# In the last two attention tiles: half of the first mixings' results in the scores' PSUM banks, and the copy of the second mixing's result one slot earlier, between two exponentials

## The chip, the core and the metric

The kernel runs on one core of a Trainium2 chip. The core has five engines that run side by side, each through its own list of instructions in order: PE (TensorE, matrix products, results into PSUM), DVE (VectorE), ACT (ScalarE), POOL (GpSimd) and SP, which here only issues DMAs. They wait for each other by semaphores. The metric is the device time of one execution in microseconds (us); less is better.

## What is computed

Attention with "talking heads" for 4 batches, 12 heads, 448 positions of 64 elements, and then an MLP with SiLU over the 1792 tokens:

```python
scores = scale * np.matmul(q, k.transpose(0, 1, 3, 2))
scores = np.einsum('bhij,hg->bgij', scores, w_pre)      # first mixing of the heads
scores = scores - np.max(scores, axis=-1, keepdims=True)
attn = np.exp(scores)
attn = attn / (np.sum(attn, axis=-1, keepdims=True) + 1e-09)
attn = np.einsum('bhij,hg->bgij', attn, w_post)         # second mixing
out = np.matmul(attn, v)
h = x @ w_in                                            # x: out, one row per token
g = h * (1.0 / (1.0 + np.exp(-h)))
return g @ w_out
```

## The kernel before, in words

A *tile* is up to 120 query positions of one batch; there are 16 tiles, four to a batch. A tile is worked in *groups* of 10 positions times 12 heads, 12 groups in most tiles and 10 in the last of a batch: 184 groups, 0 to 183. The last two tiles are groups 162 to 173 and 174 to 183.

The loop over the groups is written out as a software pipeline, and the order of its lines is the order of the instructions on each engine; nothing is reordered later. One pass of the loop is a *slot*, i. Groups go in pairs (i, i + 1 with i even), and below "pair i" means this pair. In an even slot the order of the calls is:

- `mix_pair` for pair i + 4 (line 399): 8 matmuls `pp<-g,wpre` on PE, the first mixing of the scores, into two PSUM banks. In the kernel before these come from the pool `ps_p`, which has two banks, so each mixing needs the banks of the pair before it.
- In the last tile (slots from `n_last` = 174) the row maxima `nm<-pp` of both groups (line 405, DVE); in earlier tiles they come a few lines later in the same slot.
- `put_pair` of pair i - 2 (line 446, ACT): one copy `at<-pa` of the result of the second mixing, from the only buffer `pa` for it into the tile's attention matrix.
- `norm_pair` of pair i + 2: a reciprocal on DVE (line 422) and two scalings `wr<-wpost,r` on POOL (line 425).
- the exponential `e<-pp,nm` of group i + 4 (line 409, ACT).
- work spread over the slots by tables: `scores` (line 339, PE, copied out by ACT and DVE at 344 and 346), `values` (line 368, PE, `po<-at,v`, copied out by ACT at 375). The scores and the values take their banks from `ps_m`, four banks used in turn. The last scores are made in slot 162; after it `values` runs in slots 164, 167, 171, 177, 180 and 182.
- `mix_pair_again` for pair i (line 437): 64 small matmuls `pa<-wr,e` on PE into `pa`. It needs `pa` copied out, so the `put_pair` of pair i - 2.

In the odd slot i + 1: the exponential of the pair's second group (i + 5), the copies of `po`, and `bound_sums` (line 418, POOL), which starts what the next slot's `norm_pair` needs.

Beside this the MLP's weights are converted in the background, in units (`convert`). In nearly every pair of slots from 166 on one unit runs: in the even slot DVE L86 and, for the unit before, DVE L63 and POOL L66 (and for every second unit POOL L69 to L72); in the odd slot ACT L90, after the exponential, and then DVE L92 and L93, which use what L90 writes. They come on DVE ahead of the next even slot's row maxima.

In the last slots the MLP begins: L650 and L652 (ACT, DVE) split its first operands in two, L615 and L616 (ACT, POOL) do so for its weights, and in slot 182 its first two products `ph<-op` (line 645) run on PE, one ahead of the last `mix_pair_again` and one behind it. The second needs the weights of the second L616.

Of the kernel before, what the change touches and what calls it, by code (L numbers as in the profile page):

```python
# [103 lines left out]
def talking_heads_then_silu_mlp(  # L104
# [63 lines left out]
    def pool(name, bufs, stack=ctx, **kw):  # L168
        return stack.enter_context(tc.tile_pool(name=name, bufs=bufs, **kw))
# [7 lines left out]
    ps_m = pool("ps_m", 4, late_ps, side="right", space=PSUM)  # L177
# [3 lines left out]
    ps_p = pool("ps_p", 2, mixing, space=PSUM)  # L181
# [5 lines left out]
    def pair(p, tag, dtype=F32R):  # L187
        return p.tile([128, 2, S], dtype, name=tag, tag=tag)
# [7 lines left out]
    def bank(p, name):  # L196
        if p is ps_a:
            turns.append(name)
            return pa[:, len(turns) % 2]
        return p.tile([128, 512], F32, name=name, tag="bank")  # L200
# [158 lines left out]
    def values(n, first_pair, pairs):  # L359

        b, ti = seq[n]
        t0, m, _ = tiles[ti]
        po = bank(banks[0], "po")
        for c in range(pairs):
            h = 2 * (first_pair + c)
            for j in range(NJ):
                for i in range(2):
                    nc.tensor.matmul(  # L368
                        po[i * D:(i + 1) * D, c * m:(c + 1) * m], lhsT=vs[b, h][:, i, j, :],
                        rhs=ats[n][:, j, h + i, :m], start=(j == 0), stop=(j == NJ - 1))  # L370

        def take():
            for c in range(pairs):
                p = first_pair + c
                nc.scalar.copy(
                    out=xt[p // HC, b % 2, p % HC][:, b // 2, t0:t0 + m].rearrange("p (x y s) -> p x y s", y=R, s=2),
                    in_=po[:, c * m:(c + 1) * m].rearrange("p (x s y) -> p x y s", y=R, s=2))
        return [(take, None)]
# [71 lines left out]
    seq = [(b, ti) for b in range(B) for ti in range(len(tiles))]  # L450
# [5 lines left out]
    groups, first = [], []  # L456
# [12 lines left out]
    def put(i, what, *args, lead=0, w=0.0):  # L469
        i = max(i, 0)  # L470
        (early if lead else work)[max(i - lead, 0)].append((what, args))
        sent[max(i - lead, 0)] += w

    NE = 3
    for n in range(1, len(seq)):
        p0, p1 = first[n - 1], first[n]
        spread = (0, 0, 0, 0, 2, 2) if n == 1 else (-6, -5, -4, -2, -1, 0) if p1 - p0 == 12 else (-6, -5, -4, -3, -2, -1)
        for h in range(0 if n > 1 else 2 * NE, H, 2):
            i = p0 + spread[h // 2]
# [7 lines left out]
    for n, (b, ti) in enumerate(seq):  # L487
# [12 lines left out]
        if ti == 0:  # L500
            for h in range(0, H, 4):
                put(first[n] + ((5, 6, 8) if n else (15, 16, 18))[h // 4], load_v_quad, b, h, lead=2, w=1.8)
    n_last = first[len(seq) - 1]
    lighter = set()
    for n in range(2, len(seq) - 1):
        slots = range(first[n], first[n + 1])
# [96 lines left out]
    def load_part(j):  # L603
        src, k, p = parts[j]
        if src is wo_dram:
            for _ in conv:
                pass
        n = p.stop - p.start
        raws[j] = box["w"].tile([128, 4, 128], F32R, name="wl", tag="wl", bufs=WB)[:, :n]
        nc.sync.dma_start(out=raw(raws[j]), in_=src[:, p, k])  # L610

    def ready_part(j):
        wl = raws.pop(j)
        wh = box["w"].tile([128, 4, 128], F32R, name="wh", tag="wh", bufs=WB)[:, :wl.shape[1]]
        nc.scalar.copy(out=wh, in_=raw(wl))  # L615
        nc.gpsimd.tensor_sub(out=wl, in0=raw(wl), in1=raw(wh))  # L616
        ready[j] = wh, wl
# [14 lines left out]
    def product(s, p):  # L632

        kind, k, u, a = steps[s]
        if kind == "o":
            return product_out(s, p)
        nk = HC
        todo = []
        for n in range(nk):
            wh, wl = (x[:, (a * nk + n) % 4] for x in ready[part_of(kind, k, a * nk + n)])  # L640
            x = ops[u][n]
            todo += [(0, wh, x[:, 0]), (1, wh, x[:, 1]), (2, wl, x[:, 0])]
        todo.sort(key=lambda t: t[0])
        for n, (_, w, x) in enumerate(todo):
            nc.tensor.matmul(p[:, :T], lhsT=w, rhs=x, start=(n == 0), stop=(n == len(todo) - 1))  # L645

    def halve(src, dst):

        hi, lo = (dst[:, 0], dst[:, 1]) if not isinstance(dst, tuple) else dst
        nc.scalar.copy(out=hi, in_=src)  # L650
        yield
        nc.vector.tensor_sub(out=lo, in0=src, in1=raw(hi))  # L652
# [42 lines left out]
    for i in range(len(groups) + 1):  # L695
        g, new, old = at(i), at(i + LEAD), at(i - 1)
        if i == n_last:
            early_p.close()
            xw = pool("xw", 1)
            box["w"] = pool("w", 1)  # L700

            ops[0] = [pair(xw, f"op0{c}") for c in range(HC)]
            splits = [halve(xs[0][0, 0, c], ops[0][c]) for c in range(HC)]
        for what, args in early[i]:
            what(*args)
        fresh = [new, at(i + LEAD + 1)] if new and i % 2 == 0 else []
        if fresh:
            new.mix_pair(fresh[1], ps_p)
        if i >= n_last:
            for x in fresh:  # L710
                x.top()
        if new and i % 2:
            new.exp(at(i + LEAD - 1).s[:, 1:2])
        for take, _ in done:
            take()
        if 0 < i < len(groups) and i % 2 == 0:
            at(i - 2).put_pair()
        for take, _ in later:
            if take:
                take()  # L720
        if i == len(groups) - 1:
            old.put_pair()
        if any(what is scores for what, _ in work[i]):
            for _, take in later:
                if take:
                    take()
            later = []
        if i < n_last:
            for x in fresh:
                x.top()  # L730
        for _, take in later:
            if take:
                take()
        if i % 2 and at(i + 3):
            at(i + 3).bound_sums()
        if i % 2 == 0 and at(i + 2):
            at(i + 2).norm_pair(at(i + 3))
        if scaled:
            next(conv)
            scaled = False  # L740
        for take in lows:
            take()
        if fresh:
            new.exp_first()
        later, done, highs, lows = [], [], [], []
        for what, args in sorted(work[i], key=lambda x: order.index(x[0])):
            while len(later) + len(done) + len(lows) + 1 + (what is scores) > 4:
                for take in (done or later).pop(0):
                    if take:
                        take()  # L750
            new_takes = what(*args) or []
            if what in (prep_q, prep_k):
                highs += [take for take, _ in new_takes]
                lows += [take for _, take in new_takes]
                new_takes = []
            if what is scores:
                while len(later) > 1:
                    for take in later.pop(0):
                        if take:
                            take()  # L760
            (done if what is values else later).extend(new_takes)
        for take in highs:
            take()
        if i == len(groups) - 2:
            phs.append(bank(ps_m, "ph"))
            product(0, phs[0])
        if g and i % 2 == 0:
            g.mix_pair_again(at(i + 1))
        if i == len(groups) - 2:
            phs.append(bank(ps_m, "ph"))  # L770
            product(1, phs[1])
        if i >= n_last:
            if i >= n_last + 2 and splits:
                if next(splits[0], 1):
                    splits.pop(0)
            if n_last + 2 <= i < n_last + 2 + WB:
                load_part(i - n_last - 2)
        if i in lighter:
            scaled = next(conv, None)
        if i in (len(groups) - 5, len(groups) - 3):  # L780
            ready_part(len(ready))
# [7 lines left out]
    for h in (0, HH):  # L789
        ready_part(len(ready))  # L790
        banks[:] = [(ps_m, ps_h)[h // HH]]
        new = values(len(seq) - 1, h // 2, HC)[0]
# [166 lines left out]
```

## Time and profile before

| | us |
|---|---|
| time, median of 3 runs | 857.35 (852.56 to 858.68) |
| profiled execution, time | 857.05 |
| profiled execution, span | 855.3 |
| PE busy in the span | 811.6 (95%) |
| DVE busy | 625.6 (73%) |
| ACT busy | 511.0 (60%) |
| POOL busy | 428.5 (50%) |

All times of rows are microseconds from the start of the span; 1.75 us of the profiled execution lie outside it. An L with a number is a line of the kernel, and `out<-in` names the tiles that an instruction writes and reads. "[x <-E t Ln]" behind a row says that the engine sat idle for x us ahead of it, until engine E had done the instruction of line n on tile t. The attention takes the time up to some 435 us, the MLP the rest.

### The profile page before, as it was taken

To read this page: it belongs to the slowest core of one execution; us is meant where nothing else is said; L and a number is where in the kernel's file an instruction comes from. 1 tells how busy PE (TensorE), PEld (TensorE's weight loads), DVE (VectorE), ACT (ScalarE), POOL (GpSimd) and SP (SyncE) were. 2 spreads that over 40 slices of the span, in tenths; PEclk is the share of its full clock that TensorE was granted. 3 is DMA by queue.
4 is the path that set the end of the run, shared out by engine and by line. 5 is a ranking of instruction groups with operands and counts; after the bars stand their busy time and mean duration, and the time that the engine had idled before them with its cause. 6 is when DMAs were issued, how large, how long until landed. Compare 5 with 4: busy or idle time off the path is not lost.

```text
span 855.3 us, 27555 instructions
## 1 busy us (share of the span) xinstructions
PE 811.6 (95%) x11148; PEld 661.6 (77%) x11148; DVE 625.6 (73%) x1137; ACT 511.0 (60%) x1114; POOL 428.5 (50%) x693
## 2 busy tenths in 40 slices
PE   7898999799998999999899999999999999999997
PEld 5455666467665666666599999998989999999996
DVE  5553867467775777675778798999998888787343
ACT  4675878578886888787756554224676533433330
POOL 6131536355553554563877588457644435433440
PEclk9899999899999999999999999999999999999999
DMA  8668678887788786875535346335522122111133
GB/s 172 185 181 190 189 207 232 211 207 208 209 238 225 217 216 203 239 232 160 182 117 177 124 148 200 109 105 154 154 71 66 56 73 90 52 55 56 56 121 130
DMA packets 156839, 132.90 MB, mean 155 GB/s; under 512 B 52164, under 2 KB 150448, under 8 KB 156712
## 3 DMA queue, kind: packets, MB, share of 16 engines
q1 hardware_dynamic: 154339, 129.29, 53.3%
q8 instruction: 88, 1.44, 0.7%
q10 hardware_dynamic: 1956, 1.19, 0.6%
q0 software_dynamic: 416, 0.66, 0.3%
q14 instruction: 40, 0.32, 0.1%
HBM read 64.01 MB, written 27.53 MB: 107 GB/s over the span
## 4 chain that ended last, share of the span: by engine, by line
PE 71%; DVE 12%; DMA 6%; ACT 4%; issue 3%; POOL 2%; SPq 1%; ACTq 1%; DVEq 0%; POOLq 0%
PE ph L645 17%; PE ph L629 12%; PE pt L629 9%; PE pa L437 9%; PE po L368 7%; PE pp L399 7%; PE pqk L339 7%; DMA g<-st 3%; DVE op L652 2%; ACT e L409 1%; DVE nm L405 1%; DVE g L836 1%; DVE cg L92 1%; ACT at L446 1%; DVE g L838 1%
## 5 line engine op out<-in xcount | busy, mean ns | idle before, releaser
L616 POOL TENSOR_TENSOR wl<-wl,wh 128x384 fp32r<-128x384 f32 (+1 forms) x98 | 144.1, 1487 | 124.7 <-ACT wh L615 119.7
L425 POOL TENSOR_SCALAR wr<-wpost,r 128x60 f32<-128x60 f32 x184 | 72.7, 409 | 179.2 <-DVE r L422 131.6
L405 DVE TENSOR_REDUCE nm<-pp 128x1 f32<-128x448 f32 x184 | 106.1, 619 | 75.1 <-PE pp L399 74.6
L645 PE MATMUL ph<-op,wh 128*128 128x448 f32 x672 | 155.6, 367 | 2.7 <-DVE g L846 1.8
L409 ACT ACTIVATE e<-pp,nm 128x448 f32<-128x448 f32 x184 | 115.6, 633 | 46.6 <-DVE nm L405 44.0
L645 PEld LDWEIGHTS ph<-op,wh 128*128 128x128 f32 x672 | 125.3, 188 | 15.6 <-DVE g L846 2.1
L437 PEld LDWEIGHTS pa<-wr,e 64*64 64x64 f32 (+1 forms) x5888 | 96.4, 131 | 47.4 <-issue 29.2
L437 PE MATMUL pa<-wr,e 64*64 64x60 f32 (+1 forms) x5888 | 108.5, 218 | 16.7 <-ACT at L446 7.4
L66 POOL TENSOR_TENSOR cg<-cw,cg 128x256 f32<-128x256 f32 x96 | 75.7, 788 | 73.8 <-DVE cw L63 70.6
L399 PE MATMUL pp<-g,wpre 64*64 64x448 f32 x736 | 102.4, 573 | 8.3 <-ACT e L409 5.6
L446 ACT COPY at<-pa 120x960 f32<-120x960 f32 x92 | 90.0, 978 | 3.5 <-PE pa L437 3.5
L368 PE MATMUL po<-at,v 120*64 120x120 f32 (+1 forms) x1536 | 89.0, 271 | 2.1 <-DMA v<-in_v 1.2
L368 PEld LDWEIGHTS po<-at,v 120*64 120x64 f32 x1536 | 78.5, 141 | 15.4 <-issue 6.6
L645 PE MATMUL ph<-op,wl 128*128 128x448 f32 x336 | 86.6, 366 | 0.0
L344 DVE COPY st<-pqk 120x448 f32<-120x448 f32 (+1 forms) x89 | 54.8, 617 | 34.3 <-PE pqk L339 19.2
L90 ACT ACTIVATE cg<-cg,ebias 128x256 int32<-128x256 int32 x96 | 49.6, 517 | 39.8 <-DVE cg L86 38.6
L615 ACT CAST wh<-wl 128x384 fp32r<-128x384 f32 (+1 forms) x98 | 52.1, 556 | 33.1 <-DMA wl<-wi_dram 26.1
L92 DVE SCALAR_TENSOR_TENSOR cg<-cw,cg 128x256 int32<-128x256 int32 x96 | 55.4, 577 | 18.0 <-ACT cg L90 17.7
L645 PEld LDWEIGHTS ph<-op,wl 128*128 128x128 f32 x336 | 63.0, 188 | 5.5 <-POOL wl L616 0.5
L339 PEld LDWEIGHTS pqk<-kh,qh 64*120 64x120 f32 (+1 forms) x186 | 18.8, 174 | 43.2 <-issue 15.9
L346 ACT COPY st<-pqk 120x448 f32<-120x448 f32 (+1 forms) x89 | 48.1, 540 | 6.5 <-DMA g<-st 4.9
L399 PEld LDWEIGHTS pp<-g,wpre 64*64 64x64 f32 x736 | 23.2, 133 | 33.2 <-ACT e L409 14.5
(141 smaller groups left out, 1621.9 us busy)
## 6 DMA issues: line engine op xcount, KB each, us to landing
g<-st SPq DMA_DIRECT2D x132, 210.0 KB
cw<-in_moe_w_in SPq DMA_DIRECT2D x48, 256.0 KB
cw<-in_moe_w_out SPq DMA_DIRECT2D x48, 256.0 KB
wi_dram<-cg SPq DMA_DIRECT2D x24, 448.0 KB
wo_dram<-cg SPq DMA_DIRECT2D x24, 448.0 KB
wl<-wi_dram SPq DMA_DIRECT2D x42, 256.0 KB
wl<-wo_dram SPq DMA_DIRECT2D x56, 192.0 KB
g<-st SPq DMA_DIRECT2D x48, 175.0 KB
```

What stands on the lines that cost most here:

```text
L66: nc.gpsimd.tensor_mul(out=e, in0=m, in1=e)
L339: nc.tensor.matmul(ps[i][:m, :S], lhsT=q_[rows, hh, :m], rhs=k_[rows], start=(step == 0), stop=(step == 2))
L368: nc.tensor.matmul(po[i * D:(i + 1) * D, c * m:(c + 1) * m], lhsT=vs[b, h][:, i, j, :], rhs=ats[n][:, j, h + i, :m], start=(j == 0), stop= ...
L399: nc.tensor.matmul((self, other)[r].p[HP * c:HP * (c + 1), :S], lhsT=wpre[rows], rhs=gs[self.n][rows, o // R + c * np + p, :], start=True, ...
L405: nc.vector.tensor_reduce(out=self.nm, in_=self.p[:GP, :S], axis=AX.X, op=ALU.max, negate=True)
L409: nc.scalar.activation(out=self.e, in_=self.p[:GP, :S], func=AF.Exp, bias=self.nm, scale=1.0, accum_out=sums)
L425: nc.gpsimd.tensor_scalar(out=g.wr, in0=wpost.rearrange("p g i -> p (g i)"), scalar1=r[:, i:i + 1], scalar2=1.0, op0=ALU.mult, op1=ALU.mult)
L437: nc.tensor.matmul(half[64 * c:64 * c + m, s, j * GH:(j + 1) * GH], lhsT=g.e[rows, j * JT + c * JH:j * JT + c * JH + m], rhs=g.wr[rows], s ...
L446: nc.scalar.copy(out=ats[self.n].rearrange("p j g t -> p (j g) t")[:, :, o:o + 2 * R].rearrange("p x (c i) -> p x c i", i=RH), in_=pa[:KV] ...
L616: nc.gpsimd.tensor_sub(out=wl, in0=raw(wl), in1=raw(wh))
L629: nc.tensor.matmul(p[:, :W2], lhsT=x, rhs=w, start=(g == 0 and n == 0), stop=(g == FG - 1 and n == len(todo) - 1))
L645: nc.tensor.matmul(p[:, :T], lhsT=w, rhs=x, start=(n == 0), stop=(n == len(todo) - 1))
```

## The change

Two things change for slots from 162 (`n_calm`). The first mixing of every second pair (slots 162, 166, 170, 174 and 178) writes to two banks of `ps_m` and no longer of `ps_p`. And `put_pair` of pair i is no longer called in slot i + 2 but in slot i + 1, ahead of the exponential of the second group.

```diff
--- before.py
+++ after.py
@@ -500,7 +500,7 @@
         if ti == 0:
             for h in range(0, H, 4):
                 put(first[n] + ((5, 6, 8) if n else (15, 16, 18))[h // 4], load_v_quad, b, h, lead=2, w=1.8)
-    n_last = first[len(seq) - 1]
+    n_calm, n_last = first[-3:-1]
     lighter = set()
     for n in range(2, len(seq) - 1):
         slots = range(first[n], first[n + 1])
@@ -705,7 +705,9 @@
             what(*args)
         fresh = [new, at(i + LEAD + 1)] if new and i % 2 == 0 else []
         if fresh:
-            new.mix_pair(fresh[1], ps_p)
+            new.mix_pair(fresh[1], ps_m if i >= n_calm and i % 4 else ps_p)
+        if i % 2 and i > n_calm:
+            old.put_pair()
         if i >= n_last:
             for x in fresh:
                 x.top()
@@ -713,13 +715,11 @@
             new.exp(at(i + LEAD - 1).s[:, 1:2])
         for take, _ in done:
             take()
-        if 0 < i < len(groups) and i % 2 == 0:
+        if 0 < i <= n_calm and i % 2 == 0:
             at(i - 2).put_pair()
         for take, _ in later:
             if take:
                 take()
-        if i == len(groups) - 1:
-            old.put_pair()
         if any(what is scores for what, _ in work[i]):
             for _, take in later:
                 if take:
```

On ACT, from the exponentials of pair 172 to those of pair 176, the kernel before has this (`at<-pa` is `put_pair`, here of pairs 168 and 170):

```order
L409 ACTIVATE e,s<-pp,nm 128x448 x2
L90 ACTIVATE cg<-cg,ebias 128x256
L446 COPY at<-pa 120x48x20
L409 ACTIVATE e,s<-pp,nm 128x448 x2
L90 ACTIVATE cg<-cg,ebias 128x256
L375 COPY x_128<-po 128x120
L375 COPY x_129<-po 128x120
L446 COPY at<-pa 120x48x20
L409 ACTIVATE e,s<-pp,nm 128x448 x2
```

The changed kernel has this in the same place:

```order
L409 ACTIVATE e,s<-pp,nm 128x448
L446 COPY at<-pa 120x48x20
L409 ACTIVATE e,s<-pp,nm 128x448
L90 ACTIVATE cg<-cg,ebias 128x256
L409 ACTIVATE e,s<-pp,nm 128x448
L446 COPY at<-pa 120x48x20
L409 ACTIVATE e,s<-pp,nm 128x448
L90 ACTIVATE cg<-cg,ebias 128x256
L375 COPY x_128<-po 128x120
L375 COPY x_129<-po 128x120
L409 ACTIVATE e,s<-pp,nm 128x448
```

The copy now stands between the two exponentials of a pair, and L90 comes behind all three.

On DVE the order is the same in both kernels; this is the changed one, from the end of slot 171 to slot 174 (`nm<-pp` are the row maxima that the exponentials need):

```order
L92 SCALAR_TENSOR_TENSOR cg<-cw,cg 128x256
L93 TENSOR_SCALAR cw<-cw 128x256
L405 TENSOR_REDUCE nm<-pp 128x1 x2
L422 RECIPROCAL r<-r 128x2
L86 TENSOR_SCALAR cg<-cw 128x256
L63 SCALAR_TENSOR_TENSOR cw<-cw 128x256
L92 SCALAR_TENSOR_TENSOR cg<-cw,cg 128x256
L93 TENSOR_SCALAR cw<-cw 128x256
L405 TENSOR_REDUCE nm<-pp 128x1 x2
```

Nothing moved here: L92 and L93, which follow ACT's L90, stand ahead of each pair's row maxima.

On ACT near the end, from the first exponential of pair 182, the kernel before has this:

```order
L409 ACTIVATE e,s<-pp,nm 128x448
L650 CAST op_8365<-x_119 128x448
L409 ACTIVATE e,s<-pp,nm 128x448
L90 ACTIVATE cg<-cg,ebias 128x256
L615 CAST wh<-wl 128x512
L446 COPY at<-pa 120x48x20
L650 CAST op_8366<-x_120 128x448
```

And the changed kernel:

```order
L409 ACTIVATE e,s<-pp,nm 128x448
L650 CAST op_8366<-x_119 128x448
L446 COPY at<-pa 120x48x20
L409 ACTIVATE e,s<-pp,nm 128x448
L90 ACTIVATE cg<-cg,ebias 128x256
L615 CAST wh<-wl 128x512
L650 CAST op_8367<-x_120 128x448
L446 COPY at<-pa 120x48x20
```

Here the copy of pair 178 moved ahead of the last exponential, of L90 and of the first L615. PE's, POOL's and SP's orders are the same in both kernels; what changes on PE is which bank the first mixings write, and so whose reading they wait for.

## Rows read from the trace of the kernel before

**Rows 1.** Windows: us, busy time of each engine (count), granted clock, DMA share, GB/s.
```profile
393.00:404.00 11.00, 10.03 (x286) 7.05 (x285) 5.42 (x16) 8.26 (x21) 3.43 (x10) 1.00 0.58 175
404.00:423.00 19.00, 16.19 (x463) 10.61 (x467) 15.15 (x38) 14.42 (x36) 14.60 (x30) 1.00 0.50 157
423.00:435.00 12.00, 10.71 (x257) 9.32 (x250) 7.45 (x17) 8.71 (x20) 10.97 (x18) 1.00 0.66 207
450.00:600.00 150.00, 149.05 (x730) 136.14 (x729) 138.39 (x229) 68.67 (x135) 100.67 (x114) 1.00 0.47 145
```

**Rows 2.** The chain that ended last, 405 to 408 us: start us, us, what.
```profile
405.53 0.41 ACT cg L90
405.96 0.70 DVE cg L92
406.69 0.43 DVE cw L93
407.12 0.54 DVE nm L405
```

**Rows 3.** Timeline of ACT, last two tiles: start us, us, instruction [idle before <-releaser].
```profile
404.19 0.64 ACT L409 ACTIVATE e<-pp,nm 128x448 f32<-128x448 f32 x1 [0.37 <-DVE nm L405]
...
404.81 0.63 ACT L409 ACTIVATE e<-pp,nm 128x448 f32<-128x448 f32 x1
...
405.42 0.50 ACT L90 ACTIVATE cg<-cg,ebias 128x256 int32<-128x256 int32 x1
405.82 0.95 ACT L446 COPY at<-pa 120x960 f32<-120x960 f32 x1
407.77 0.64 ACT L409 ACTIVATE e<-pp,nm 128x448 f32<-128x448 f32 x1 [0.99 <-DVE nm L405]
...
422.97 0.64 ACT L409 ACTIVATE e<-pp,nm 128x448 f32<-128x448 f32 x1 [0.66 <-DVE nm L405]
...
425.07 0.61 ACT L615 CAST wh<-wl 128x512 fp32r<-128x512 f32 x1
425.58 0.96 ACT L446 COPY at<-pa 120x960 f32<-120x960 f32 x1
426.43 0.57 ACT L650 CAST op<-x 128x448 fp32r<-128x448 f32 x1
```

**Rows 4.** Timeline of DVE: the conversion's last two steps on two passes.
```profile
402.01 0.44 DVE L92 SCALAR_TENSOR_TENSOR cg<-cw,cg 128x256 int32<-128x256 int32 x1 [1.01 <-ACT cg L90]
402.49 0.30 DVE L93 TENSOR_SCALAR cw<-cw 128x256 int32<-128x256 int32 x1
...
409.66 0.50 DVE L92 SCALAR_TENSOR_TENSOR cg<-cw,cg 128x256 int32<-128x256 int32 x1 [0.24 <-ACT cg L90]
410.19 0.72 DVE L93 TENSOR_SCALAR cw<-cw 128x256 int32<-128x256 int32 x1
```

**Rows 5.** Timeline of PE, last two tiles.
```profile
409.80 0.98 PE L399 MATMUL pp<-g,wpre 64*64 64x448 f32 x8
411.35 1.16 PE L437 MATMUL pa<-wr,e 64*64 64x60 f32 x64 [0.56 <-ACT at L446]
412.35 1.59 PE L399 MATMUL pp<-g,wpre 64*64 64x448 f32 x8
...
426.68 1.16 PE L437 MATMUL pa<-wr,e 64*64 64x60 f32 x64 [1.29 <-POOL cg L66]
...
434.01 0.78 PE L645 MATMUL ph<-op,wl 128*128 128x448 f32 x3
```

**Rows 6.** Timeline of POOL: the first two weight subtractions at line 616.
```profile
426.94 1.27 POOL L616 TENSOR_TENSOR wl<-wl,wh 128x512 fp32r<-128x512 f32 x1
...
432.52 1.29 POOL L616 TENSOR_TENSOR wl<-wl,wh 128x512 fp32r<-128x512 f32 x1
```

**Rows 7.** Windows early in the program.
```profile
66.00:70.00 4.00, 2.29 (x76) 1.46 (x72) 2.06 (x5) 3.11 (x8) 0.82 (x3) 1.00 0.92 182
70.00:78.00 8.00, 7.46 (x124) 4.74 (x124) 2.46 (x6) 3.42 (x9) 0.82 (x3) 0.79 0.99 196
```

## The prediction

> **What bounds the kernel now.** I read four views in this order: the busy time by windows, to see how much there is to win; the chain of work that ended last, to see what sets the pace in the last two tiles; the timelines of ACT and DVE there, for durations and idle time; and the timelines of PE and POOL at the step into the MLP.
>
> The windows [rows 1] give the ceiling. From 393 to 435 us PE is busy 10.03 + 16.19 + 10.71 = 36.93 of 42 us, so 5.1 us are idle. Some waiting hides in busy time: a first mixing without a wait shows 0.98 us, one that waits between its matmuls 1.59 [rows 5]; in slots 164, 170, 174 and 176 they show 1.47 to 1.59, 2.2 us too much in all. So the change can win some 7 us at most, 0.8% of the time. What it wins or loses there stays: from 450 to 600 us PE is busy 149.05 of 150 us [rows 1], so there is no slack in the MLP that could absorb a shift.
>
> What holds PE back is not one thing. Before `pa` it waits some 0.5 us for the copy at L446, as at 411.35 [rows 5], and in `pp` for exponentials to leave the banks of `ps_p`. Those are the two waits that the change is about. But the chain that ended last runs elsewhere in this stretch: ACT L90, DVE L92, DVE L93, DVE `nm`, then ACT's exponential, and round again [rows 2]. The timeline of ACT shows the same ring [rows 3]: exponential at 404.19, the second at 404.81, L90 at 405.42, then 0.99 us idle until the row maxima are there, and the next pair's exponential at 407.77. From there to pair 182 at 422.97 it turns five times in 18.78 us, 3.76 us each. PE, whose products for a pair without `values` are one mixing of 0.98 us and one of 1.16 us, could go faster; this ring could not.
>
> **The change, part by part.**
>
> *First mixings in the scores' banks.* No instruction is added. PE no longer waits for the exponentials of the pair before: at most 0.6 us in a pair that waited [rows 5]. New is that the mixing, the last `scores` and `values` wait for whoever read the `ps_m` banks last. I place this at 0 to 0.4 us, once, where the scores of slot 162 now need ACT's copy of the previous scores; later every bank was read some 4 us or more before. The win leads nowhere by itself: from pair 174 on, the row maxima stand on DVE behind L93 and start right after it, without a wait for PE [rows 2]. An earlier `pp` finds DVE's queue in front of it.
>
> *The copy between two exponentials.* It takes 425.58 to 426.43 = 0.85 us of ACT [rows 3]. Before, it lay behind L90, in the 0.99 us in which ACT waited anyway: it cost the ring nothing. Now it stands ahead of the second exponential, and L90 behind that. So L90 comes 0.85 us later in each turn, and with it L92, L93, the row maxima and the next exponential. What is queued behind the copy on ACT: the second exponential, L90, the copies of `po`. Who waits for these: DVE for L90, POOL's L418 for the second exponential's sum. The copy itself rarely waits for PE: the second mixing that it reads ends well before the first exponential, because PE's 1.16 + 0.98 us, and the `values` where there are any, fit into a turn.
>
> Five turns: 5 x 0.85 = 4.25 us. One relief: in two of the five, where L92 and L93 met POOL's L66, they took 0.50 + 0.72 us, while at 402 us, away from it, they took 0.44 + 0.30 us [rows 4]; from L92's start to L93's end these are 1.25 and 0.78 us, so 0.47 us less. A DVE step that comes 0.85 us later falls behind L66. 2 x 0.47 = 0.94 us. If the other three turns, where POOL still has L69 to L72 to do, escaped it as well (1.16 us from L92's start to L93's end in [rows 2], so 0.38 less each), the sum would be 1.1 us smaller; I leave them as they are. The Trainium skill (SBUF — State Buffer, section "Who interferes with whom") says that a DVE instruction with two SBUF inputs and a GpSimd instruction that reads SBUF exclude each other for a whole instruction; by it, those three turns would even lose up to a POOL instruction each if they met it from its start. The rows agree only in that both steps come out longer beside POOL, by less than half a microsecond.
>
> So the first exponential of pair 182 comes 4.25 - 0.94 = 3.3 us late. Ahead of the ring, in slots 162 to 170, PE has only 0.97 us of idle time in 11 [rows 1]; what is gained and lost there I put at 0, between -1 and +0.5.
>
> *What is won back at the end.* Pair 182 is the last; its copies are on the path. Before, the copy of pair 178 started 425.58 - 422.97 = 2.61 us after that exponential, behind L650, the second exponential, L90 and L615, and PE's `pa` of pair 180 began at 426.68, right after it ended at 426.54 [rows 3, 5] (the row names a POOL instruction that ended at about the same time; the copy is the one that `pa` cannot do without). Now only the exponential (0.62) and one L650 (0.57) are ahead: 1.2 us instead of 2.6, so 1.4 us come back. By this route PE is 3.3 - 1.4 = 1.9 us late.
>
> The other route goes through POOL. The first L615 now has the copy ahead of it: exponential 0.62, L650 0.57, copy 0.85, exponential 0.62, L90 0.4 come to 3.0 us after the exponential of pair 182, against 425.07 - 422.97 = 2.1. So it is 3.3 + 0.9 = 4.2 us late; it used to end at 425.68, and POOL's L616 took it up at 426.94, so 1.3 us of that are slack and 2.9 us arrive. From there POOL works without a gap to the second L616, which ends at 433.81 [rows 6], and PE's last three products of `ph` start at 434.01 [rows 5]: slack 0.2. By this route PE is 2.7 us late.
>
> **The sum.** Between 1.9 and 2.7 us later; I take 2.3, the middle, since POOL's instructions there are stretched by DVE and may shrink a little when the two shift. On the profiled execution that is 857.05 + 2.3 = 859.35; the median stands 0.3 above that execution, so 859.7.
>
> **The rivals.**
>
> *The waits go and nothing replaces them.* ACT's idle 0.99 us ahead of an exponential [rows 3] is larger than the copy, and PE gets both its waits back. Against it: that idle time lies behind L90, and the copy now lies in front of L90. It holds if L90 to the row maxima can shrink, say if DVE's steps escape POOL in all turns and the earlier part wins its 1 us. All 7 us would give 850; half of them, which I take for this rival, 853.5.
>
> *The clock falls.* PE's work from pair 172 to 176 would be 2 x (1.16 + 0.98) us in two turns of 4.4, about half the time, with a pause of over 2 us ahead of each `pa`. Early in the program, four microseconds with PE busy 2.29 of 4 ended in a pause, and the granted clock over the next eight was 0.79 [rows 7]: part of them at 1.2 GHz and not 2.4, a loss of 8 x 0.21 = 1.7 us where PE was the bound. One such fall near 420 us adds that to my sum: 861.4. If it stayed at 1.2 GHz from 411 us to the start of the MLP, PE's products there, some 21 us (10.71 of the third window and 12/19 of the 16.19 of the second [rows 1]), would take 42, where 24 + 2.3 us are there by my sum: 16 us more, 875. It decides this way from the point where the clock stays down through the pairs with `values`, which PE bounds. For it speaks the sparser PE; against it that the window from 404 to 423 us, with 16.19 of 19 busy, was granted 1.00 throughout, and that the `values` of slots 171 and 177 keep PE dense on both sides. The Trainium skill (TensorE: Matmul & The Clock Gate, section "HAM oscillation — how this bites in real kernels") warns of idle gaps that return in each iteration; by it this rival would be likelier the longer the gaps get. No row here shows gaps of this size in this pattern.
>
> *It does nothing.* The ring's loss and the win at the end cancel, when the DVE steps escape POOL in most turns: 857.5.
>
> **How the numbers follow.** My forecast has 0.60, the waits' removal 0.18, nothing 0.12, the falling clock 0.10, of which 0.02 for the case that it stays down. 1% of the time, 8.6 us, is about what a measurement of this kernel can tell from no change (three runs of before lie 6 us apart). No case but the clock that stays down leaves that band upwards, and only the full 7 us with a low median could leave it downwards: faster 0.02, same 0.94, slower 0.04. My own bounds are 857.6 (PE's route, all meetings escaped, the early slots' 1 us won) to 861.5 (no relief, POOL's route, the early slots' 0.5 lost). With the first rival below and one fall of the clock above, and the spread of medians on top, the range is 853.5 to 863.5.
>
> **What would show it right.** In the changed kernel's timeline the copies stand between two exponentials, the pairs from 172 to 182 start their exponentials some 4.4 us apart (3.76 before), L90 to the next exponential stays at 2 to 2.4 us, the row maxima again start right behind L93, and the mixings `pp` are all near 0.98 us, while PE's waits ahead of `pa` grow to over 2 us in slots without `values`. The first `ph` would start some 2 us later and the second end near 437.5. I am wrong if the exponentials come 3.8 us apart or less, or if DVE's row maxima wait for PE again.

## The result, and the profile after

Over 13 runs each, in turn on the same chips, the changed kernel took 863.97 us in the median (858.46 to 868.47), the kernel before 862.15 us (852.56 to 869.21). The ratio is 1.0056, with a 95% interval of 1.0031 to 1.0081: slower by 0.3 to 0.8%. A second measurement on another chip, with 12 runs of the change and 35 of before, gave 1.0003 (0.9971 to 1.0036). The ratios leave out runs in a slower state that some executions show; over all the runs listed the means are 863.91 and 861.44 us, 2.5 us apart, in the first and 862.92 and 862.27 us, 0.65 us apart, in the second. Each of these differences has about 2.5 to 3 us of uncertainty, so the times put the change between no loss and some 5 us of loss, and no closer. The measured median, 863.97 us, lies 4.3 us above the predicted 859.7 and just outside the range of 853.5 to 863.5.

The profiled execution of the change took 863.48 us (span 861.8). The place of the change is compared by a measure of its own, because the rest of the program varies by more: the **tail**, from the start of the second mixing of pair 162 to the start of the last `values`, which follow the MLP's second product; and the **step**, the mean distance of the first exponentials of the pairs from 172 to 182. Before, the tail goes from 392.99 to 434.72 = 41.73 us, and the step is 3.76 us. The timeline of PE before:

```profile
389.43 1.16 PE L437 MATMUL pa<-wr,e 64*64 64x60 f32 x64
...
392.99 1.16 PE L437 MATMUL pa<-wr,e 64*64 64x60 f32 x64
...
434.72 4.34 PE L368 MATMUL po<-at,v 120*64 120x100 f32 x96
```

In the timeline of PE in the changed kernel the tail goes from 395.87 to 439.68 = 43.81 us, 2.08 us more:

```profile
391.90 1.16 PE L437 MATMUL pa<-wr,e 64*64 64x60 f32 x64
...
395.08 0.45 PE L339 MATMUL pqk<-kh,qh 64*100 64x448 f32 x2 [0.31 <-ACT st L346]
...
395.87 1.11 PE L437 MATMUL pa<-wr,e 64*64 64x60 f32 x62
...
413.58 0.55 PE L399 MATMUL pp<-g,wpre 64*64 64x448 f32 x2
...
413.64 0.97 PE L399 MATMUL pp<-g,wpre 64*64 64x448 f32 x6
416.87 1.11 PE L437 MATMUL pa<-wr,e 64*64 64x60 f32 x63 [2.26 <-ACT at L446]
...
421.26 1.98 PE L437 MATMUL pa<-wr,e 64*64 64x60 f32 x64 [1.70 <-ACT at L446]
423.17 2.58 PE L368 MATMUL po<-at,v 120*64 120x120 f32 x32
...
439.07 0.68 PE L645 MATMUL ph<-op,wl 128*128 128x448 f32 x2 [0.74 <-POOL wl L616]
439.68 4.34 PE L368 MATMUL po<-at,v 120*64 120x100 f32 x96
```

Against [rows 5]: the first mixing of slot 174, which waited in the middle (1.59 us before, at 412.35), now takes 1.03 us, from 413.58 to 414.61, and in its place PE stands 2.26 us idle ahead of `pa`, waiting for the copy.

The tail leaves a part of the change out. The first mixing of slot 162 already writes to the scores' banks, and behind it the last `scores` wait 0.31 us for ACT's copy L346. From the second mixing of pair 160 to that of pair 162 it takes 395.87 - 391.90 = 3.97 us, where it was 392.99 - 389.43 = 3.56: 0.41 us more, just ahead of the tail. It is 3.97 to 3.99 us in the ten profiles of this document with the new banks and 3.56 to 3.58 in the four without. So the change costs 2.08 + 0.41 = 2.49 us in this stretch.

At the end of the tail, PE waits 0.74 us for POOL's second L616, which used to be through 0.2 us before it was needed. The durations of 1.98 and 2.58 at 421 and 423 us, which are 1.16 and 1.86 elsewhere, are the clock. The windows of PE there (us, then busy time of PE, PEld, DVE, ACT and POOL with counts, the granted clock, the DMA share and GB/s) show it at 0.50, its level of 1.2 GHz, after a stretch in which PE was busy 1.74 of 4 us:

```profile
414.00:418.00 4.00, 1.74 (x76) 1.17 (x72) 2.34 (x8) 2.60 (x6) 2.21 (x5) 0.98 0.21 70
418.00:420.00 2.00, 1.57 (x9) 0.10 (x2) 1.97 (x6) 0.46 (x1) 1.41 (x4) 0.50 0.44 130
...
422.00:424.00 2.00, 2.00 (x56) 1.89 (x50) 1.79 (x6) 0.57 (x2) 0.05 (x1) 0.50 0.76 215
```

The timeline of ACT answers to [rows 3]:

```profile
406.57 0.63 ACT L409 ACTIVATE e<-pp,nm 128x448 f32<-128x448 f32 x1 [1.13 <-DVE nm L405]
...
407.20 0.95 ACT L446 COPY at<-pa 120x960 f32<-120x960 f32 x1
408.03 0.65 ACT L409 ACTIVATE e<-pp,nm 128x448 f32<-128x448 f32 x1
...
408.65 0.51 ACT L90 ACTIVATE cg<-cg,ebias 128x256 int32<-128x256 int32 x1
410.97 0.64 ACT L409 ACTIVATE e<-pp,nm 128x448 f32<-128x448 f32 x1 [1.80 <-DVE nm L405]
...
428.43 0.63 ACT L409 ACTIVATE e<-pp,nm 128x448 f32<-128x448 f32 x1 [1.49 <-DVE nm L405]
...
429.51 0.96 ACT L446 COPY at<-pa 120x960 f32<-120x960 f32 x1
...
431.38 0.62 ACT L615 CAST wh<-wl 128x512 fp32r<-128x512 f32 x1
```

Between two first exponentials, 406.57 and 410.97, now lie the copy, the second exponential, L90 and 1.80 us of waiting for the row maxima: 4.40 us, where it was 3.58. The last pair's comes at 428.43, so the step is (428.43 - 406.57) / 5 = 4.37 us. The first L615 follows 2.95 us after it (2.10 before). The timeline of DVE answers to [rows 4] and [rows 2]:

```profile
409.20 0.66 DVE L92 SCALAR_TENSOR_TENSOR cg<-cw,cg 128x256 int32<-128x256 int32 x1 [1.62 <-ACT cg L90]
409.89 0.43 DVE L93 TENSOR_SCALAR cw<-cw 128x256 int32<-128x256 int32 x1
410.24 1.14 DVE L405 TENSOR_REDUCE nm<-pp 128x1 f32<-128x448 f32 x2
...
413.60 0.52 DVE L92 SCALAR_TENSOR_TENSOR cg<-cw,cg 128x256 int32<-128x256 int32 x1 [1.62 <-ACT cg L90]
414.15 0.35 DVE L93 TENSOR_SCALAR cw<-cw 128x256 int32<-128x256 int32 x1
```

L92 waits 1.62 us for L90, and the row maxima start right behind L93 without a wait for PE. L92 and L93 take 1.12 us from start to end in one turn and 0.90 or less in the next. The chain of work that ended last now carries the copy itself, between the exponential and the next L90:

```profile
411.69 0.85 ACT at L446
412.54 0.62 ACT e L409 x2
413.17 0.41 ACT cg L90
...
413.60 0.53 DVE cg L92
...
414.36 1.21 DVE nm L405 x2
```

### The profile page after: what moved, and what is told of

It reads as the page before. It is cut to its first block, busy times and chain, and to the rows that moved or that the text cites. A ratio compares the mean times of both kernels' runs of the same rounds, so it can differ in the third digit from the quotient of the medians.

```text
span 861.8 us, 27559 instructions
## 1 busy us (share of the span) xinstructions
PE 813.2 (94%) x11148; PEld 663.4 (77%) x11148; DVE 624.2 (72%) x1137; ACT 509.6 (59%) x1114; POOL 427.9 (50%) x693
## 4 chain that ended last, share of the span: by engine, by line
PE 70%; DVE 12%; ACT 5%; DMA 5%; issue 3%; POOL 2%; ACTq 1%; SPq 0%; DVEq 0%; POOLq 0%
PE ph L645 17%; PE ph L629 12%; PE pt L629 9%; PE pa L437 8%; PE pqk L339 7%; PE pp L399 7%; PE po L368 7%; DMA g<-st 3%; DVE nm L405 2%; ACT at L446 2%; DVE cg L92 2%; DVE op L652 1%; ACT e L409 1%; DVE g L836 1%; DVE g L838 1%
## 5 line engine op out<-in xcount | busy, mean ns | idle before, releaser
L616 POOL TENSOR_TENSOR wl<-wl,wh 128x384 fp32r<-128x384 f32 (+1 forms) x98 | 144.9, 1495 | 126.2 <-ACT wh L615 117.3
L437 PE MATMUL pa<-wr,e 64*64 64x60 f32 (+1 forms) x5888 | 110.3, 221 | 19.0 <-ACT at L446 11.1
L66 POOL TENSOR_TENSOR cg<-cw,cg 128x256 f32<-128x256 f32 x96 | 75.2, 784 | 73.3 <-DVE cw L63 70.1
L90 ACT ACTIVATE cg<-cg,ebias 128x256 int32<-128x256 int32 x96 | 49.6, 517 | 40.8 <-DVE cg L86 40.6
L92 DVE SCALAR_TENSOR_TENSOR cg<-cw,cg 128x256 int32<-128x256 int32 x96 | 55.5, 578 | 24.2 <-ACT cg L90 23.9
L615 ACT CAST wh<-wl 128x384 fp32r<-128x384 f32 (+1 forms) x98 | 52.0, 555 | 33.0 <-DMA wl<-wi_dram 26.1
L339 PE MATMUL pqk<-kh,qh 64*120 64x448 f32 (+1 forms) x186 | 47.2, 467 | 5.5 <-issue 2.5
L346 ACT COPY st<-pqk 120x448 f32<-120x448 f32 (+1 forms) x89 | 47.9, 539 | 6.4 <-PE pqk L339 3.4
```

The lines of the kernel that those rows point to most:

```text
L66: nc.gpsimd.tensor_mul(out=e, in0=m, in1=e)
L92: nc.vector.scalar_tensor_tensor(out=e, in0=hi, scalar=-2 ** 31, in1=e, op0=ALU.bitwise_and, op1=ALU.bitwise_or)
L339: nc.tensor.matmul(ps[i][:m, :S], lhsT=q_[rows, hh, :m], rhs=k_[rows], start=(step == 0), stop=(step == 2))
L437: nc.tensor.matmul(half[64 * c:64 * c + m, s, j * GH:(j + 1) * GH], lhsT=g.e[rows, j * JT + c * JH:j * JT + c * JH + m], rhs=g.wr[rows], s ...
```

## Experiments

All were timed against the kernel before on the same chip. Tail and step are from one profiled execution each, taken as above; differences of less than half a microsecond in the tail are not read by themselves, since they were not repeated except for the change itself. To compare a kernel with the new banks to one without, 0.41 us ahead of the tail have to be added to its tail. "Both rings" in the table are the one through L90 and a second one through POOL's queue, which e4 brings to light.

| kernel | tail us | step us | ratio to before (95%) |
|---|---|---|---|
| before | 41.73 | 3.76 | |
| changed | 43.81 | 4.37 | 1.0056 (1.0031 to 1.0081) |
| e1 changed again | 43.71 | 4.35 | 1.0003 (0.9971 to 1.0036) |
| e2 banks only | 41.30 | 3.76 | 0.9994 (0.9964 to 1.0025) |
| e3 copy only | 47.55 | 4.34 | 1.0034 (0.9997 to 1.0072) |
| e4 changed, row maxima first | 40.98 | 3.80 | 0.997 (0.9934 to 1.0005) |
| e5 before, row maxima first | 42.45 | 3.85 | 0.9998 (0.9967 to 1.0029) |
| e6 changed, copy twice | 50.95, not compared | 5.21 | 1.0074 (1.0041 to 1.0107) |
| e7 changed, L90 ahead of the copy | 41.74 | 3.69 | 1.0012 (0.9974 to 1.005) |
| e8 banks, row maxima first | 41.81 | 3.88 | 1.0042 (1.0008 to 1.0076) |
| e9 changed, both rings open | 39.67 | 3.42 | 1.0002 (0.998 to 1.0025) |
| e10 before, both rings open | 42.00 | 3.81 | 1.0017 (0.9993 to 1.0041) |
| e11 changed, small sum on DVE | 43.65 | 4.27 | 1.0037 (1.0012 to 1.0062) |
| e12 banks, both rings open | 41.17 | 3.73 | 1.0016 (0.9985 to 1.0048) |

**e1, the change again.** No edit.

> The changed kernel once more. Measured by the stretch from the start of the second mixing of pair 162 to the start of the last values behind the MLP's second product (41.73 us before, 43.81 us after in the first two profiles, called the tail below), and by the step of the first exponentials from pair 172 to pair 182 (3.76 us before, 4.37 after). Theory of the ring: the tail is again 43.5 to 44.3 us, the step 4.3 to 4.5, and the whole program is longer by the tail's 2 us alone, +0.25%. Rival, that the change also costs time outside the tail: +0.5% or more again, with a tail of no more than 44.3 us.

Tail and step came back within 0.1 us of the first profile, so the 2 us are the change's and not the run's. The kernel before was profiled once, but the five kernels below with the copy in its old place lie at 41.17 to 42.45 us. The whole program did not come out 0.5% slower again; the interval holds the tail's 0.25%.

**e2, banks only.**

```diff
-            new.mix_pair(fresh[1], ps_p)
+            new.mix_pair(fresh[1], ps_m if i >= n_calm and i % 4 else ps_p)
```

> Only the first mixings go to the scores' banks, the copy stays in its old place. Theory of the ring: the step stays at 3.7 to 3.8 us and the tail at 41.0 to 41.8 us, since the waits of the first mixings were not what set the pace; the mixings themselves show 0.98 us. Rival, that the banks are what costs (waits for the scores' and values' readers): tail 43 us or more.

The step is 3.76 us to the hundredth. The tail is 0.4 us shorter, and 0.41 us were lost just ahead of it: from the second mixing of pair 160 on it is 437.87 - 392.59 = 45.28 us, against 45.29 before. Alone, the banks neither cost nor win in these profiles.

**e3, copy only.** The changed kernel with

```diff
-            new.mix_pair(fresh[1], ps_m if i >= n_calm and i % 4 else ps_p)
+            new.mix_pair(fresh[1], ps_p)
```

> Only the copy moves between the two exponentials, all first mixings stay in their own two banks. Theory of the ring: step 4.3 to 4.6 us, tail 43.5 to 45 us, as long as the change as a whole or a little longer. Rival, that the copy's place costs nothing and the banks do: tail 41.7 us.

The step is as expected, but the tail is 47.55 us, 3.7 us longer than with the banks and beyond both expectations. PE's timeline shows why:

```profile
397.10 0.92 PE L399 MATMUL pp<-g,wpre 64*64 64x448 f32 x2
399.04 0.98 PE L399 MATMUL pp<-g,wpre 64*64 64x448 f32 x6 [1.02 <-ACT e L409]
...
402.71 0.92 PE L399 MATMUL pp<-g,wpre 64*64 64x448 f32 x2
404.60 0.60 PE L399 MATMUL pp<-g,wpre 64*64 64x448 f32 x3 [0.97 <-ACT e L409]
```

In most slots the first mixing now does two matmuls and then waits for the second exponential of the pair before, which stands behind the copy, which itself waits for PE's second mixing. From pair 162 to the exponential of pair 172 this takes 14.6 us, against 10.7 in the changed kernel and 11.2 before. So the banks are what makes the moved copy bearable; the two parts are not independent.

**e4, the ring opened in the changed kernel.** L92 and L93 of a slot are held back until the next slot's row maxima have been issued:

```diff
+        if owed:
+            next(conv, None)
+            owed = False
         if i % 2 and at(i + 3):
             at(i + 3).bound_sums()
...
+        opened = scaled
         if scaled:
             next(conv)
...
         if i in lighter:
-            scaled = next(conv, None)
+            if i % 2 and i > n_last - 12 and opened:
+                owed = True
+            else:
+                scaled = next(conv, None)
```

> The changed kernel with one order turned on DVE: from slot 163 on, the conversion's last two steps (L92, L93) come behind the next pair's row maxima and no longer ahead of them, so that the ring through L90 is open. Theory of the ring: the step falls below 3.8 us though the copy is where the change put it, the tail is 38 to 40.5 us, and the program is 1 to 3 us faster than before. Rival, that the copy's place itself delays the path (second exponential, POOL's scalings, the single buffer): step and tail stay at 4.3 and 43 us or more.

The step falls from 4.36 to 3.80 us and the tail from 43.8 to 40.98, with the copy where the change put it; both stay a little above what was expected. That is the test of the ring: the copy's place costs only as long as L90, behind it, holds up the row maxima. The time points the same way, though its interval just reaches 1. The steps are uneven: 2.49, 4.09, 2.67, 3.96 and 5.81 us. In the first four, something else comes last every second pair. DVE's timeline names it:

```profile
404.92 0.17 DVE L422 RECIPROCAL r<-r 128x2 f32<-128x2 f32 x1 [1.59 <-POOL r L418]
405.00 0.27 DVE L86 TENSOR_SCALAR cg<-cw 128x256 int32<-128x256 int32 x1
...
405.54 1.16 DVE L405 TENSOR_REDUCE nm<-pp 128x1 f32<-128x448 f32 x2
```

The reciprocal waits 1.59 us for POOL's small sum L418, which stands behind L69 to L72 in POOL's queue; L86 is behind the reciprocal, and the next row maxima behind that. The last step is long for another reason, which the timelines of PE and DVE show:

```profile
412.49 1.78 PE L437 MATMUL pa<-wr,e 64*64 64x60 f32 x64 [2.35 <-ACT cg L90]
414.20 2.81 PE L368 MATMUL po<-at,v 120*64 120x120 f32 x32
...
417.98 1.16 DVE L405 TENSOR_REDUCE nm<-pp 128x1 f32<-128x448 f32 x2 [2.81 <-PE pp L399]
```

The granted clock was 0.50 there (413 to 415 us), `pa` and `values` took 1.78 and 2.81 us in place of 1.16 and 1.86, and the row maxima waited for the first mixing behind them. With the ring open PE came last there, so by estimate some 1.6 us of this tail are the clock's (0.62 + 0.95). In e8 and e9 the clock stayed at 1.00 throughout the tail.

**e5, the ring opened in the kernel before.** The edit of e4 on the kernel before.

> The kernel before, without any part of the change, with L92 and L93 of the conversion behind the next pair's row maxima from slot 163 on. Theory of the ring: it was what set the pace before too, so the step of the first exponentials falls from 3.76 to 3.3 to 3.7 us, and the tail from 41.7 to 39 to 41 us; now exponentials that leave the two banks of the first mixing, and POOL's scalings, come last. Rival, that PE's waits for banks and copy set the pace before: step and tail unchanged within 0.3 us.

Step and tail did not fall: 3.85 and 42.45 us. The rival's forecast of "unchanged" was the better one here. The ring was where the chain of before ran, but other waits stood right behind it. The timelines of DVE and PE of this run show them:

```profile
414.32 1.16 DVE L405 TENSOR_REDUCE nm<-pp 128x1 f32<-128x448 f32 x2 [0.70 <-PE pp L399]
...
420.25 1.59 PE L399 MATMUL pp<-g,wpre 64*64 64x448 f32 x8
...
426.51 1.16 PE L437 MATMUL pa<-wr,e 64*64 64x60 f32 x64 [1.52 <-POOL cg L66]
```

The row maxima, no longer behind L93, wait for PE instead. First mixings still take 1.59 us, since they wait inside for the exponentials to leave two banks, and `pa` waits 1.52 us; the POOL instruction it is put down to is not one that `pa` reads, while ACT's copy, which it needs, ended at 426.37.

**e6, twice the suspected cost.**

```diff
         if i % 2 and i > n_calm:
             old.put_pair()
+            if i < n_last + 7:
+                old.put_pair()
```

> The changed kernel with each copy that stands between two exponentials made twice (same data to the same place). Theory of the ring: every turn gets the copy's 0.85 us once more, so the step goes from 4.36 to 5.1 to 5.3 us, and the tail from 43.8 to 47 to 48.5. Rival, that ACT has idle time there which takes a copy in (1.1 to 1.8 us ahead of each first exponential): step and tail grow by less than 0.3 and 1 us.

```profile
417.26 0.63 ACT L409 ACTIVATE e<-pp,nm 128x448 f32<-128x448 f32 x1 [1.10 <-DVE nm L405]
...
417.88 1.94 ACT L446 COPY at<-pa 120x960 f32<-120x960 f32 x2
...
422.46 0.63 ACT L409 ACTIVATE e<-pp,nm 128x448 f32<-128x448 f32 x1 [1.61 <-DVE nm L405]
```

Each turn grew by 5.21 - 4.36 = 0.85 us, the duration of the copy, although ACT then idles 1.6 us ahead of the next exponential. The profiled execution took 879.44 us, 10.7 us more than the median of this kernel's runs, so only the step inside this short stretch is used and not the tail, which was forecast at 47 to 48.5 us and is 50.95.

**e7, L90 ahead of the copy.**

```diff
+        if scaled and i % 2 and i > n_calm:
+            next(conv)
+            scaled = False
         if i % 2 and i > n_calm:
             old.put_pair()
```

> The changed kernel with ACT's L90 moved ahead of the copy, right behind the first exponential of the pair, from slot 163 on; DVE's order as in the changed kernel. Theory of the ring: copy and second exponential are out of the ring, the step falls to 3.0 to 3.9 us (whichever of L86, which waits for POOL, and PE comes last), the tail to 39.5 to 41.5 us. Rival, that the delay of the second exponential by the copy, and not of L90, is what costs: step stays at 4.2 us or more.

Step 3.69 us: with the copy and the second exponential out of the ring, the delay is gone, whichever way the ring is opened. The steps alternate again, 3.14 and 4.20, with L90 itself waiting 1.03 us for L86 every second time. The tail, 41.74 us, a little above the expected 41.5, is back by the 2 us that the change had added, and would be shorter but for PE's 1.27 us wait for POOL's second L616 at its end.

**e8, banks and row maxima first, copy in the old place.** The edits of e2 and e4.

> First mixings in the scores' banks as in the change, copy in its old place, L92 and L93 behind the row maxima. With the ring open in both, this against the same with the moved copy (tail 40.98 us) tells what the copy's place is worth for PE: if the wait for the copy matters once the ring is open, the tail is 41.3 to 43 us; if POOL's scalings and the products come last, it is 40 to 41.3 us. In the MLP the clock falls by chance if it is the same here as in the others: 0.96 or 1.00 in the 40 us from 180 us behind the tail.

41.81 us of tail against 40.98 with the moved copy, of which some 1.6 us are the low clock's. With the ring open the copy's new place is rather a gain than a loss, by 0.8 us in these two profiles; e9 and e12 ask this again. The ratio of the whole program, 1.0042 (1.0008 to 1.0076), excludes 1 although the tail is as before: what lies outside the tail moves it, so the ratios are not used to tell these kernels apart.

**e9, both rings open in the changed kernel.** The edit of e4, and

```diff
         if i % 2 == 0 and at(i + 2):
+            if i > n_last - 12:
+                at(i + 2).bound_sums(nc.vector)
             at(i + 2).norm_pair(at(i + 3))
```

with the call on POOL left out in those slots.

> The changed kernel with the row maxima ahead of L92 and L93, and with the small sum L418 on DVE ahead of its reciprocal and no longer on POOL behind L69 to L72. What is asked: what set the pace once the ring through L90 was open (steps of 2.5 and 4.0 us in turn, 3.80 in the mean). Theory of a second ring, POOL's L72, L418, DVE's reciprocal, L86, L90 or POOL's scalings: now steps of 2.6 to 3.6 us, mean 3.0 to 3.5, tail 38 to 40 us, faster than before by 1.5 to 3.5 us. Rival, that PE's own order (its waits for the copy) holds the mean at 3.8: no change against 40.98 us of tail.

Step 3.42 and tail 39.67 us, as expected: 4.1 us less than the change, 2.1 less than before (1.65 with the 0.41 us ahead of the tail). The steps are still uneven (2.51 and 4.23 at first); PE now waits 1 to 1.6 us for POOL's scalings, ahead of which L69 to L72 stand. Against e4 the move of the small sum wins 1.3 us of tail, which is no more than the low clock cost there; that it wins anything by itself is not shown. The whole program shows nothing of the 2 us: 1.0002 (0.998 to 1.0025), so this is no version to recommend on its time.

**e10, both rings open in the kernel before.** The edits of e9 on the kernel before.

> The kernel before with the same two turns (row maxima ahead of L92 and L93; L418 on DVE), the copy and the banks as before. With the row maxima turned alone its step was 3.85 and its tail 42.45 us, no better than before. Theory of the second ring: step 3.2 to 3.6, tail 39.5 to 41. Rival, that the two banks of the first mixings hold it: step 3.7 or more, tail 41.5 or more.

The rival was right: 3.81 and 42.00 us, no gain. Without the second set of banks and the earlier copy, the two queues are not what keeps the old order at its pace.

**e11, only the small sum on DVE.** The last edit of e9 on the changed kernel.

> The changed kernel with only L418 moved to DVE; L92 and L93 stay ahead of the row maxima. Theory of the ring through L90, which the copy lengthened: the second ring does not bind here, so the step stays at 4.3 to 4.45 us and the tail at 43 to 44. Rival, that POOL's queue is what holds the changed kernel: step under 4.1.

4.27 and 43.65 us: in the changed kernel POOL's queue is not the bound, the ring is. The step is a shade under the expected 4.3.

**e12, banks and both rings open, copy in the old place.** The edits of e2 and e9 on the kernel before.

> First mixings in the scores' banks, the copy in its old place, row maxima ahead of L92 and L93, L418 on DVE. Against the same with the copy between the exponentials this tells what the copy's place is worth for PE once both rings are open: if the wait for the copy matters, this tail is longer by 0.5 to 2 us; if not, the two agree within 0.5 us.

41.17 us against 39.67 with the copy moved: 1.5 us for the copy's place, as in e8 against e4 (0.8 us) in sign. So what the change is after exists; it is to be had only where the row maxima do not wait for the L90 that stands behind the copy.

## Why the prediction was right and wrong

*The ring and the copy in it: right.* The prediction had the first exponentials 4.4 us apart, the row maxima right behind L93, `pp` near 0.98 us and waits of over 2 us ahead of `pa`. They came 4.37 us apart, with 0.98 to 1.03 us as long as the clock was up, and waits of 2.26 and 1.70 us, the second a little shorter than forecast. That this is the cause, and not only a coincidence in the chain, is shown by e6 (twice the copy, 0.85 us more per turn) and by e4 and e7 (two ways of opening the ring, and the delay goes).

*The size in the stretch: right.* Predicted 1.9 us by PE's route and 2.7 by POOL's, 2.3 in the sum; measured 2.08 us in the tail and, again, 1.98 (43.71 - 41.73), or 2.49 and 2.40 with the 0.41 us ahead of it. By its terms: the scores' wait in slot 162 was put at 0 to 0.4 us and came as 0.41; up to the first exponential of pair 172 the tail then won 0.50 us (10.70 against 11.20), so the early slots came out near the 0 that was forecast. The five turns lost 21.86 - 18.78 = 3.08 us (3.3 forecast). From the first exponential of pair 182 to the end of the tail it takes 11.25 us against 11.75, so 0.50 us came back: POOL's route (0.6) and not PE's (1.4). Both marks of it are visible: the copy of pair 178 starts 1.08 us after the last pair's exponential (429.51 - 428.43; predicted 1.2), and PE waits for POOL's second L616, which ends at 439.03, before the last of `ph`'s products go on at 439.07.

*The relief by POOL: right.* Predicted 0.47 us in two turns of five. These are the first exponentials before, between 407.77 and 422.97 [rows 3]:

```profile
411.57 0.64 ACT L409 ACTIVATE e<-pp,nm 128x448 f32<-128x448 f32 x1 [0.38 <-DVE nm L405]
...
415.15 0.63 ACT L409 ACTIVATE e<-pp,nm 128x448 f32<-128x448 f32 x1 [0.99 <-DVE nm L405]
...
418.93 0.64 ACT L409 ACTIVATE e<-pp,nm 128x448 f32<-128x448 f32 x1 [1.08 <-DVE nm L405]
```

The steps were 3.58, 3.80, 3.58, 3.78 and 4.04 us and are now 4.40, 4.18, 4.40, 4.02 and 4.86. Three turns grew by 0.82 us, near the whole copy, and the second and fourth by 0.38 and 0.24: 0.47 and 0.61 us less than the 0.85. (At 402 us L92 still ran beside L66 for 0.16 us, so that row is not quite free of it.)

*"An earlier `pp` finds DVE's queue in front of it": right alone, and incomplete.* e2 bears it out: nothing won, from pair 160 on. What the working did not price is that the moved copy without the banks would cost 5.8 us and not 2 (e3).

*"This ring could not go faster; PE could": wrong as a statement on the kernel before.* e5 and e10 open the ring there and nothing is won. The row of DVE that stands behind L93 in [rows 4] shows how near the next limit was:

```profile
410.83 1.16 DVE L405 TENSOR_REDUCE nm<-pp 128x1 f32<-128x448 f32 x2
```

PE's mixing, which these row maxima read, had ended at 409.80 + 0.98 = 410.78 [rows 5], 0.05 us earlier; in the other four turns it ended 0.39 to 0.68 us ahead of them. So in the old order at least PE's first mixing comes in within 0.7 us of the ring, and behind it stand the copy and POOL's queue. How near those are was not measured one by one. It did not hurt the sum, since lengthening one of several nearly equal limits makes it the bound at once; it would have ruined a forecast of what opening it brings.

*The clock: its rival happened, at no price there.* The granted clock fell to 0.50 around 420 us in both profiles of the change (rows above), for which 1.7 us were set aside. PE was not the bound in that stretch; the step after it, 4.02 us, is no longer than its like: 4.03 us in e3, where the clock stayed at 1.00. The Trainium skill (TensorE: Matmul & The Clock Gate, section "HAM oscillation — how this bites in real kernels") warns of idle gaps of PE that return in each iteration, behind which the next products start at the lower clock. The trace agrees for the gaps of 2.26 and 1.70 us here; in e7, with gaps of 1.26 and 2.29 us, the clock stayed at 1.00. What the fall costs depends on who comes last: nothing here, some 1.6 us in e4, where PE did.

*The time: wrong, and this is the step that failed.* "the median stands 0.3 above that execution, so 859.7": the level to which the change was added, and a range that was laid around it, with a spread from the same three runs. Those three (852.56, 857.35 and 858.68) lay low: with ten more the median of the kernel before is 862.15 us, 4.8 us higher, over a spread of 17 us, and in the three later measurements 35 runs of it each gave 862.03, 861.32 and 860.61. The forecast of +2.3 us on 862.15 would have been 864.5, against 863.97 measured.

"What it wins or loses there stays" failed too, as a statement on one execution: the two profiled executions are 863.48 - 857.05 = 6.4 us apart, of which the tail is 2.1, the part ahead of it 2.9 (0.41 of it the change's) and the part behind it 1.5. From the span's start to pair 162, where nothing differs but the 0.41 us, the profiles of the kernels here run from 388.4 us (e12) to 400.5 us (e5), that of e6 aside. And behind the tail it takes 420.58 us before and 422.12 us with the change. The windows of the MLP, 4 us each, show where 1.5 us of this go. Before, from some 188 us behind the tail:

```profile
622.72:626.72 4.00, 2.26 (x11) 2.11 (x12) 3.85 (x8) 2.82 (x6) 2.32 (x3) 1.00 0.00 0
626.72:630.72 4.00, 4.00 (x22) 3.70 (x21) 4.00 (x9) 2.77 (x7) 2.38 (x4) 1.00 0.00 0
```

And in the changed kernel:

```profile
627.68:631.68 4.00, 2.33 (x7) 2.07 (x8) 3.86 (x9) 2.88 (x6) 2.25 (x3) 0.73 0.00 0
631.68:635.68 4.00, 4.00 (x18) 3.67 (x17) 4.00 (x9) 2.77 (x7) 2.39 (x4) 0.85 0.00 0
```

In both, PE waits 1.8 us there for DVE. Only in the second does the clock fall behind it, 4 x 0.27 + 4 x 0.15 = 1.7 us of full speed. It fell there in 7 of the 8 profiles with the copy between the exponentials (not in e9) and in 2 of the 6 with it in its old place (e8 and e12). That leans towards the change, which would then cost another 1.5 us in the MLP, far from the place where it was made; but nothing here tests it, and 14 profiles of thirteen kernels don't settle it. It stays open.

## What to carry to other kernels

An engine's idle time says nothing of whether an instruction is free in it: find what ends that idle time, and put the new instruction behind what it waits for, not ahead of it. Here 0.85 us of copy were free behind L90 and cost 0.82 us in three turns of five ahead of it, because L90 fed the other engine's queue in which the next step's input stood. And where several waits end together, as here before the change, lengthening one costs nearly in full, while shortening one wins nothing. The size of an effect on a short stretch is better read there than in a time that varies by eight times as much, and a forecast of the time itself needs a level from more than three runs.

## What the runs showed of the hardware that was not expected

The same instructions, from the start to pair 162 (but for the bank of one mixing, 0.41 us), took between 388.4 and 400.5 us in twelve profiles, that of e6 left out, and 393.0 in that of before. That is far more than the difference looked for. Part of it goes with the clock: windows of 50 us with a granted clock between 0.90 and 1.00 lie elsewhere in each profile. And a single wait of PE of 1.8 us in an otherwise full stretch was followed by the lower clock in some executions and not in others (0.73 against 1.00 over the same 4 us).
